# Planned queue orders and slots, and a second Strassen-Winograd level on more of K, in a gated mix of a Fourier transform and a two-layer network

## The chip, the cores and the metric

One core of one Trainium2 chip runs the program. The metric is the device time of one execution in microseconds; lower is better. A time is compared by the median of several runs.

## The reference, cut to what matters

x has 2048 rows (sequence) and 1024 columns; everything is float32.

```python
g = sigmoid((x * gate_w).sum(-1, keepdims=True))
a = x @ dft_hid_re.T ; b = x @ dft_hid_im.T            # 1024 x 1024 each
y = dft_seq_re @ a - dft_seq_im @ b                    # 2048 x 2048 each
h = relu(x @ w1 + b1) ** 2                             # w1 1024 x 3584
o = h @ w2 + b2                                        # w2 3584 x 1024
out = g * y + (1 - g) * o
```

## The kernel before

There are four stages, each a large matrix product: x (the hidden transform, `x_stage`), c (the sequence transform, `c_stage`), h (the first layer in two parts of 16 and 12 tiles of the hidden width, `h_stage(0)` and `h_stage(1)`; the second part works on three-row groups), o (the second layer and the output, `o_stage`). x and h go through `wide`, c and o through `tall`.

**Precision.** A float32 factor is split into a rounded part and the rest: ScalarE writes `hi` (L221), VectorE subtracts it to give `lo` (L231). TensorE then does three matmuls, hi x hi, hi x lo and lo x hi, for each pair of tiles (L307). A row is 128x128 by 128x512. Narrow factors (256 columns) hold both in one block, `both`.

**First level.** Each stage's product is done by Strassen's scheme in Winograd's form: seven products of quarter matrices instead of eight, in the order `(1, 2, 5, 6, 3, 7, 4)`. `FACTORS` names the factors, `SUMS_L` and `SUMS_R` the sums that go into them; VectorE makes these (L173), ScalarE and VectorE evacuate PSUM and add into accumulators (L434, L440, L613, L620).

**Second level.** Some products are split once more (`twice`), others run plainly (`direct`). In `tall` K goes in steps `q` of 256, eight in c and seven in o, and `TWICE_C` and `TWICE_O` say for each product how many couples of steps take the second level; the rest of K goes direct. For a couple of four-row steps, direct is 2 q x 2 halves x 24 matmuls = 96, the second level 7 x 12 = 84. It needs more sums, more hi/lo splits and more evacuations: results of the four groups for the inner products 1, 6, 7 and 5 are added into accumulators (L492 to L531), loaded back into PSUM by ScalarE (L294), and inner products 2, 4 and 3 go on top. In `wide` `TWICE_X` and `TWICE_H` list the products that take the second level as a whole.

**Slots and queues.** SBUF is cut in 55 slots of 128x1024 float32; raw loads, sums, hi, lo and accumulators all take slots from one list. PSUM is cut in four pairs of banks. Each engine runs its queue in order, and a loop over the steps of TensorE writes the orders: at step i it issues loads for up to `LOADS` steps ahead when enough slots are free (`KEEP`, `RAWS`), makes sums and hi parts `SUMS` steps ahead and lo parts `RESTS` steps ahead, goes up to `SPREAD` steps ahead when a small running clock (`MM`, `VEC`, `LAND`, `RATE`) says VectorE would otherwise wait, and puts the last step of an accumulator `LATER` steps behind. SP queues the loads, GpSimd's queue the stores.

Of the kernel before, what the change touches and what calls it, by code (L numbers as in the profile page):

```python
# [14 lines left out]
P = 128  # L15
S, D, F = 2048, 1024, 3584
NF = F // P
SLOTS, KEEP, RAWS = 55, 5, 4
WIDE, TALL_C, TALL_O = ((1, 2, 5, 6, 3, 7, 4),) * 3
TWICE_X, TWICE_C, TWICE_O = (1, 2, 5, 3, 4), {2: 4, 3: 3, 4: 3}, {1: 2, 2: 3, 3: 3, 4: 2}  # L20
LATER = 3
# [3 lines left out]
TWICE_H = (1, 2, 5, 3, 4), (2, 5, 3, 4)  # L25
SUMS, RESTS, LOADS, SPREAD = 3, 2, 12, 9

MM, VEC, ACTS, LAND, RATE = 0.2267, (0.16, 1.067), (0.2, 0.85), 5.0, 1.5
# [14 lines left out]
def gated_mix_kernel(ctx: ExitStack, tc: tile.TileContext, x4, xn, w4, ct, w1a, w1b, w2, b1, b2, gw, out):  # L43
# [11 lines left out]
    nc = tc.nc  # L55
# [4 lines left out]
    free = deque(ctx.enter_context(tc.tile_pool(name=f"slot{i}", bufs=1)) for i in range(SLOTS))  # L60
    banks = deque(ctx.enter_context(tc.tile_pool(name=f"banks{i}", bufs=1, space=bass.MemoryType.PSUM))
                  for i in range(4))
    home = {}
    b1c = const.tile([P, NF], F32, name="b1c")
    z = const.tile([P, 16], F32, name="z")
    g = const.tile([P, 16], F32, name="g")
    b2c = const.tile([P, 8], F32, name="b2c")
    g_far = dram.tile([P, 16], F32, name="g_far")
# [4 lines left out]
    def take(name, dtype=F32):  # L73
        slot = free.popleft()
        t = slot.tile([P, 2, 512], dtype, name=name, tag="block")
        home[id(t)] = slot, t
        return t

    def give(*tiles):
        for t in tiles:  # L80
            free.append(home.pop(id(t))[0])
# [6 lines left out]
    class Near:  # L88
# [9 lines left out]
        def drop(self):  # L98
            give(self.slot)
            self.slot = None  # L100
# [19 lines left out]
    class Kept:  # L120


        def __init__(self, name):
            self.at, self.done, self.left = dram.tile([P, 2, 512], F32, name=name), False, 2
# [7 lines left out]
    class Part(Near):  # L132
# [10 lines left out]
        def room(self):  # L143
            return sum(not isinstance(b, (Near, View)) for b in self.blocks)

# [13 lines left out]
        def extra(self):  # L159
            return 0 if self.room() else 1  # L160

        def time(self):
            return VEC[0] + VEC[1] * self.width / 512 if self.op else 0.0

        def make_parts(self):
# [9 lines left out]
            give(*mine[1:])  # L175
# [13 lines left out]
        def sum(self):  # L189
            run(self.make_parts())  # L190
            return self.time()

        def rest(self):
            return 0.0

    class Operand:
# [6 lines left out]

        def room(self):
            return 0

        def extra(self):
            return (2 if self.width > 256 else 1) - (self.block.uses == 1)
# [15 lines left out]
        def sum(self):  # L224
            run(self.sum_parts())
            return 0.0
# [9 lines left out]
        def rest(self):  # L236
            run(self.rest_parts())
            return VEC[0] + VEC[1] * self.width / 512

        def used(self):  # L240
            self.uses -= 1
            if not self.uses:
                give(*((self.hi, self.lo) if self.width > 256 else (self.both,)))
# [21 lines left out]
    class Group:  # L265
# [11 lines left out]
        def ends(self):  # L277
            return (self.at + 1) % self.k == 0

        def prepare(self):  # L280

            if not all(b.begun for b in self.onto or ()):
                return
            for k in range(len(self.ps), -(-self.rows // self.per)):
                if not banks or self.per == 2 and len(banks) < -(-self.rows // 2) - k:
                    break
                self.pools.append(banks.popleft())
                t = self.pools[-1].tile([P, 2, 512], F32, name="ps", tag="ps")
                self.ps.append(t)
                if self.onto:  # L290
                    n = min(self.per, self.rows - self.per * k)
                    at = self.per * k % 2
                    b = self.onto[self.per * k // 2]
                    nc.scalar.activation(t[:, :n, :], b.slot[:, at:at + n, :], AF.Copy, scale=self.sign)  # L294
                    if self.spend and (self.per == 2 or at):
                        b.drop()

        def run(self, st, mv, by_part=False):
            self.prepare()
# [18 lines left out]
    steps, wanted, count = [], [], {}  # L318

    def step(st, mv, group):  # L320
# [3 lines left out]
        needs = 0  # L324
        count[group] = count.get(group, 0) + 1
        if count[group] % group.k == 0:
            needs += group.done[count[group] // group.k - 1][1]
        wanted.append(needs)

    stores = []  # L330
    later, now = deque(), [0]
    clock = {"pe": 10.0, "vec": 0.0, "dma": 0.0}

    def vec(t):
        clock["vec"] += t
# [77 lines left out]
    def tall(left, right, ksteps, order, second, first, target, final, last=None):  # L413
# [23 lines left out]
        def add(dst, k, ps, ends=False, src=None, sign=1):  # L437
# [3 lines left out]
            vec(VEC[0] + VEC[1])  # L441
# [19 lines left out]
        def twice(p, old, new, ends, drop, sign):  # L461
# [37 lines left out]
            def onward(dst, key, ps):  # L499

                if old:
# [4 lines left out]
                    vec(2 * (VEC[0] + VEC[1]))  # L506
# [16 lines left out]
            def five(_, ps):  # L523
                key = block(1, 1)
                add(new, block(0, 1), ps)
                if old:
# [5 lines left out]
                    vec(2 * (VEC[0] + VEC[1]))  # L532
                    tmp[0, 0].drop()
                    new[key].begun = True
                    if ends and not more:
                        new[key].done = True
                        later.append((now[0] + LATER, lambda: final(new[key], None)))
# [47 lines left out]
    def wide(left, right, rows, order, second, target, final, sign=1, onto_old=False):  # L585
# [30 lines left out]
        def add(dst, k, ps, ends=False, src=None, sign=1):  # L616
# [5 lines left out]
            vec(VEC[0] + VEC[1] * min(2, rows - 2 * k[2]) / 2)  # L622
            near.begun = True
            if ends:
                near.done = True
                later.append((now[0] + LATER, lambda: final(near, None, 1)))
# [100 lines left out]
    class Gate:  # L727
# [5 lines left out]
        def extra(self):  # L733
            return 0

        def room(self):
            return 1

# [8 lines left out]
        def sum(self):  # L747
            nc.vector.scalar_tensor_tensor(flat(self.raw), flat(self.raw), 1.0, flat(gwb.slot), op0=ALU.mult,
                                           op1=ALU.mult, accum_out=z[:, self.t:self.t + 1])
            give(self.raw)  # L750
            return VEC[0] + VEC[1]

        def rest(self):
# [5 lines left out]
            return 0.0  # L759

    class Row(Near):
# [8 lines left out]
        def extra(self):  # L770
            return 0

        def room(self):
            return 1

# [4 lines left out]
        def sum(self):  # L780
            self.done = True
            if not self.less:
                return 0.0
            nc.vector.tensor_scalar(flat(self.slot), flat(self.slot), -1.0, 1.0, op0=ALU.mult, op1=ALU.add)
            return VEC[0] + VEC[1]

        def rest(self):
            return 0.0
# [8 lines left out]
    def c_stage():  # L797
# [8 lines left out]
        def final(dst, ps):  # L806
# [3 lines left out]
            vec(VEC[0] + VEC[1])  # L810
# [8 lines left out]
    def o_stage():  # L819
# [10 lines left out]
        def last(dst, ps, k):  # L830
            i, n, c, rp = to[dst]
            e, t, add = 4 * i + 2 * rp + k, 1024 * n + 512 * c, fetched[i, n, c, rp]
            dst.slot or dst.new()
# [10 lines left out]
        def final(dst, ps):  # L844
            i, n, c, rp = to[dst]
            e, t, add = 4 * i + 2 * rp, 1024 * n + 512 * c, fetched[i, n, c, rp]
            for k in range(2):
# [4 lines left out]
            vec(2.8)  # L852
# [23 lines left out]
    for (i, n, c, rp), e in fetched.items():  # L876
        want(ends[i, n] - 7 + c if (i, n) != (1, 0) else ends[i, n] - 11 + 6 * c, e)
# [4 lines left out]
    n = len(steps)  # L882
    seen = set()
    items = []

    def need(o, k):

        o = o.base if isinstance(o, (View, Half)) else o
        if id(o) in seen or not isinstance(o, (Part, Operand, Gate, Row)):
            return  # L890
        seen.add(id(o))
        for b in [o.block] if isinstance(o, Operand) else getattr(o, "blocks", ()):
            need(b, k)
        o.need = k
        items.append(o)

    for k, (st, mv, _, also) in enumerate(steps):
        for o in (mv, st, *also):
            need(o, k)
    first = items[:4]  # L900
    assert [type(o) for o in first] == [Part, Operand] * 2
    for o in first[:2]:
        o.cuts = [(slice(k, k + 1), slice(0, 512)) for k in range(2)]
    for o in first[2:]:
        o.cuts = [(slice(0, 1), slice(0, 256)), (slice(0, 1), slice(256, 512)), (slice(1, 2), slice(0, 512))]

    w_parts, x_parts = first[0].load_parts(cycle((nc.sync,))), first[2].load_parts(iter((nc.scalar, nc.sync, nc.sync)))
    for parts in (w_parts, x_parts, x_parts, w_parts, x_parts):
        next(parts)
    run(w_parts, x_parts)  # L910
    ones = const.tile([P, P], mybir.dt.bfloat16, name="ones")
    nc.vector.memset(ones, 1.0)
    idle = banks[-1].tile([P, 2, 512], F32, name="ps", tag="ps")
    for _ in range(WARM):
        nc.tensor.matmul(idle[:, 0, :P], ones, ones, start=True, stop=True)
    run(*(o.make_parts() for o in first[::2]), *(o.sum_parts() for o in first[1::2]),
        *(o.rest_parts() for o in first[1::2]))
    for o in first:
        o.landed = 0.0

    def ready(o):
        near = [o.block] if isinstance(o, Operand) else getattr(o, "blocks", ())
        return all(b.done for b in near if isinstance(b, (Near, View)))

    loaded = summed = rested = 4
    for i in range(-SUMS, n + LATER + 2):
        start = clock["pe"] if i >= 0 else 0.0
        if 0 <= i < n:
            clock["pe"] += steps[i][2].rows * 6 * MM
        end = clock["pe"]  # L930
        ahead = sum(wanted[max(i, 0):i + 5]) + sum(o.extra() for o in items[summed:] if o.need <= i + SUMS + 1)
        while loaded < len(items) and items[loaded].need <= i + LOADS:
            o = items[loaded]
            if any(isinstance(b, Kept) and not b.done for b in getattr(o, "blocks", ())):
# [86 lines left out]
```

## Time and profile before

| | |
|---|---|
| three runs | 1882.26, 1885.99, 1886.69 us (median 1885.99) |
| profiled execution | span 1879.6 us from first to last instruction; its time with what lies around the span is not listed apart, the three runs are 2.7 to 7.1 us above the span |
| TensorE busy | 1866.2 us (99%), 8228 matmuls |
| VectorE busy | 1686.0 us (90%), 1638 instructions |
| ScalarE busy | 1044.1 us (56%) |
| granted TensorE clock | 0.999 |
| moved by DMA | 443.97 MB, 236 GB/s over the span |

A page line gives busy time, share of the span and number of instructions. In a line of a group stand line, engine, operation, out<-in, shape and count, then busy time and mean ns of one, then the idle time of the engine just before them with what ended it. In a table by stretch stand the stretch, its length, the busy time and count of TensorE, its weight loads, VectorE, ScalarE and GpSimd, the granted clock, the busy share of the DMA engines and GB/s. In the chain and the timeline stand start, length and what ran. A matmul's end is modelled (0.39 us where the next one starts 0.23 us later), so start times tell its pace.

### The profile page before, as it was taken

How to read it: one execution, taken by the hardware profiler on the slowest of the kernel's cores; microseconds unless marked ns; L12 is line 12 of the kernel's file. 1: busy time of each engine (PE TensorE's matmuls, PEld its weight loads, DVE VectorE, ACT ScalarE, POOL GpSimd, SP SyncE). 2: the span in 40 equal slices, each digit the busy share in tenths (PEclk: the TensorE clock that was granted, in tenths of full speed). 3: DMA queues.
4: the chain of work that ended last, by engine and by line, in shares of the span. 5: the costliest groups of instructions: out<-in, count | busy, mean ns of one | idle time of the engine just before them, and what ended most of it. 6: DMA issues, size and time to landing. Idle time of an engine off the chain costs nothing.

```text
span 1879.6 us, 22035 instructions
## 1 busy us (share of the span) xinstructions
PE 1866.2 (99%) x8228; PEld 1541.3 (82%) x8228; DVE 1686.0 (90%) x1638; ACT 1044.1 (56%) x1184; POOL 87.6 (5%) x162
## 2 busy tenths in 40 slices
PE   9999999999999999999999999999999999999998
PEld 7888888888888878888888888888888888887887
DVE  8997898599779898799996998799999998699898
ACT  6474563363343554366485797676977534264453
POOL 0000110000000000000000010000100000000000
PEclk9999999999999999999999999999999999999999
DMA  6732989439788379464461766536865798638971
GB/s 224 249 121 74 351 286 412 141 112 361 275 307 330 128 299 378 149 232 181 137 221 61 302 234 218 195 122 246 298 233 177 254 389 317 258 124 335 409 256 52
DMA packets 128570, 443.97 MB, mean 236 GB/s; under 512 B 14144, under 2 KB 23632, under 8 KB 128464
## 3 DMA queue, kind: packets, MB, share of 16 engines
q1 hardware_dynamic: 106560, 364.05, 53.7%
q0 software_dynamic: 21616, 78.14, 10.4%
q8 instruction: 64, 1.05, 0.2%
q10 hardware_dynamic: 288, 0.39, 0.1%
q14 instruction: 42, 0.34, 0.1%
HBM read 363.87 MB, written 78.65 MB: 235 GB/s over the span
## 4 chain that ended last, share of the span: by engine, by line
PE 94%; DVE 4%; DMA 1%; ACT 1%; issue 0%; SPq 0%; DVEq 0%; ACTq 0%
PE ps L307 94%; DVE lo L231 1%; DVE h L620 1%; DVE sum L173 1%; DMA raw<-in_x 0%; DVE u L503 0%; DMA raw<-in_w1b 0%; DMA g<-g_far 0%; DVE both L231 0%; DVE raw L173 0%; ACT ps L294 0%; ACT h L717 0%; ACT hi L221 0%; DVE o L505 0%; SPq L153 0%
## 5 line engine op out<-in xcount | busy, mean ns | idle before, releaser
L307 PE MATMUL ps<-hi 128*128 128x512 f32 x2168 | 844.3, 390 | 3.3 <-ACT hi L221 2.7
L307 PE MATMUL ps<-lo,hi 128*128 128x512 f32 x2168 | 844.1, 390 | 0.0
L307 PE MATMUL ps<-hi,lo 128*128 128x512 f32 x2168 | 843.3, 390 | 0.7 <-DVE lo L231 0.6
L221 ACT ACTIVATE hi<-raw 128x1024 fp32r<-128x1024 f32 (+2 forms) x398 | 406.8, 1037 | 370.6 <-DVE raw L173 245.7
L231 DVE TENSOR_TENSOR lo<-raw,hi 128x1024 fp32r<-128x1024 f32 (+2 forms) x398 | 468.3, 1197 | 45.5 <-ACT hi L221 28.4
L307 PEld LDWEIGHTS ps<-hi 128*128 128x128 f32 x2168 | 407.5, 188 | 89.7 <-ACT hi L221 3.5
L307 PEld LDWEIGHTS ps<-hi,lo 128*128 128x128 f32 x2168 | 407.6, 188 | 86.3 <-DVE lo L231 2.1
L307 PEld LDWEIGHTS ps<-lo,hi 128*128 128x128 f32 x2168 | 407.4, 188 | 84.4 <-DVE lo L231 0.4
L173 DVE TENSOR_TENSOR raw<-raw 128x1024 f32<-128x1024 f32 (+1 forms) x276 | 325.6, 1206 | 57.4 <-DMA raw<-in_ct 13.6
L307 PE MATMUL ps<-hi,both 128*128 128x512 f32 x1120 | 347.9, 390 | 3.1 <-ACT ps L294 3.1
L221 ACT ACTIVATE hi<-sum 128x1024 fp32r<-128x1024 f32 (+1 forms) x192 | 196.8, 1038 | 184.5 <-DVE sum L173 170.1
L231 DVE TENSOR_TENSOR lo<-sum,hi 128x1024 fp32r<-128x1024 f32 (+1 forms) x192 | 228.0, 1200 | 31.5 <-PE ps L307 18.2
L307 PEld LDWEIGHTS ps<-hi,both 128*128 128x128 f32 x1120 | 210.3, 188 | 49.4 <-ACT ps L294 5.5
L307 PE MATMUL ps<-lo,both 128*128 128x512 f32 x560 | 218.3, 390 | 0.1
L173 DVE TENSOR_TENSOR sum<-raw 128x1024 f32<-128x1024 f32 (+2 forms) x136 | 140.3, 1048 | 13.0 <-PE ps L307 9.3
L173 DVE TENSOR_TENSOR sum<-raw,sum 128x1024 f32<-128x1024 f32 (+2 forms) x102 | 112.4, 1107 | 13.3 <-PE ps L307 10.3
L307 PEld LDWEIGHTS ps<-lo,both 128*128 128x128 f32 x560 | 105.2, 188 | 22.0 <-DVE lo L231 0.6
L620 DVE TENSOR_TENSOR h<-h,ps 128x1024 f32<-128x1024 f32 x92 | 98.1, 1085 | 9.0 <-ACT u L613 7.0
L613 ACT ACTIVATE u<-ps 128x1024 f32<-128x1024 f32 x76 | 71.8, 952 | 51.6 <-PE ps L307 43.7
L294 ACT ACTIVATE ps<-u 128x1024 f32<-128x1024 f32 x79 | 76.9, 980 | 20.7 <-DVE o L848 7.1
L221 ACT ACTIVATE both<-sum 128x512 fp32r<-128x512 f32 x80 | 49.6, 625 | 58.6 <-DVE sum L173 43.6
L717 ACT ACTIVATE h<-h,b1c 128x512 f32<-128x512 f32 x112 | 74.3, 715 | 10.5 <-DVE h L620 10.2
(62 smaller groups left out, 724.2 us busy)
## 6 DMA issues: line engine op xcount, KB each, us to landing
raw<-in_ct SPq DMA_DIRECT2D x151, 512.0 KB, 6.9
raw<-h SPq DMA_DIRECT2D x134, 512.0 KB, 7.3
raw<-in_x SPq DMA_DIRECT2D x107, 512.0 KB, 4.9
raw<-in_w SPq DMA_DIRECT2D x98, 512.0 KB, 6.9
raw<-ab SPq DMA_DIRECT2D x72, 512.0 KB, 6.6
h<-h POOLq DMA_DIRECT2D x48, 512.0 KB, 5.9
raw<-in_w1a SPq DMA_DIRECT2D x36, 512.0 KB, 5.5
ab<-ab POOLq DMA_DIRECT2D x32, 512.0 KB, 6.4
```

The source lines that it names most:

```text
L173: nc.vector.tensor_tensor(self.slot[:, k, c], src[0][:, k, c], src[1][:, k, c], op=self.op)
L221: nc.scalar.activation(self.hi[:, k, c], self.block.slot[:, k, c], AF.Copy)
L231: nc.vector.tensor_tensor(self.lo[:, k, c], self.block.slot[:, k, c], self.hi[:, k, c].bitcast(F32), op=SUB)
L294: nc.scalar.activation(t[:, :n, :], b.slot[:, at:at + n, :], AF.Copy, scale=self.sign)
L307: nc.tensor.matmul(self.ps[r // self.per][:, r % self.per, :], a[:, kk, r * P:(r + 1) * P], b[:, kk, :], start=self.at == 1 and kk + n == ...
L613: nc.scalar.activation(view(near.slot, k), view(ps, k), AF.Copy, scale=float(sign))
L620: nc.vector.tensor_tensor(view(near.slot, k), view((src or dst)[k].slot, k), view(ps, k), op=ADD if sign > 0 else SUB)
L717: nc.scalar.activation(dst.slot[:, k, :], (dst.slot if ps is None else ps)[:, k, :], AF.Relu, bias=b1c[:, tile0 + k:tile0 + k + 1])
```

## The change

Which products take the second level, and on how many couples:

```diff
-TWICE_X, TWICE_C, TWICE_O = (1, 2, 5, 3, 4), {2: 4, 3: 3, 4: 3}, {1: 2, 2: 3, 3: 3, 4: 2}
+TWICE_X, TWICE_C, TWICE_O = (1, 2, 5, 3, 4), {1: 1, 2: 4, 3: 4, 4: 4}, {1: 2, 2: 3, 3: 3, 4: 3}
-TWICE_H = (1, 2, 5, 3, 4), (2, 5, 3, 4)
+TWICE_H = (1, 2, 5, 3, 4), (1, 2, 5, 3, 4)
```

The loop that wrote the queues is gone, with `KEEP`, `RAWS`, `SUMS`, `RESTS`, `LOADS`, `SPREAD` and `LATER`. The kernel now runs once against recording queues: each operation becomes an `Op` with what it reads and writes, what it must follow, and a duration by constants. Operands are made where a step first needs them; final sums are recorded at once; the gated blocks of the output stage (`fetched`) are loaded where their sum is recorded.

```diff
-MM, VEC, ACTS, LAND, RATE = 0.2267, (0.16, 1.067), (0.2, 0.85), 5.0, 1.5
+MM, MM_END, FIRST_MM = 0.2267, 0.18, 6.2
+VEC, VEC_END, ACT, ACT_END = (0.086, 1.0417e-3), 0.39, (0.11, 0.89e-3), 0.36
+ISSUE, RING, RATE, SEM, LANES = {"sync": 0.36, "scalar": 0.36, "gpsimd": 0.56}, (1.1, 1.1), 400e3, 0.06, 8
+LEAD = {"raw": 5.0, "hi": 5.0, "sum": 5.0, "out": 0.0}
-                later.append((now[0] + LATER, lambda: final(near, None)))
+                final(near, None)
+    def ready(o, engines):
...
+        for b in [o.block] if isinstance(o, Operand) else getattr(o, "blocks", ()):
+            ready(b, engines)
+        store_all()
+        o.load(engines)
+        o.sum()
+        o.rest()
+    for k, (st, mv, group, also) in enumerate(steps):
...
+        ready(mv, cycle((nc.sync,)))
+        ready(st, iter((nc.scalar, nc.sync, nc.sync)) if k == 0 else cycle((nc.sync,)))
...
+        group.run(st, mv, by_part=k == 0)
...
+    emit(tc, plan(ops, len(slots), ideal[0]), slots, pools)
```

`plan` gives each operation a time at which it is due, worked back from TensorE's matmuls at an unbroken pace, and then plays the program through: every engine takes the ready operation that is due first, a slot goes to the block whose first operation is due first less its `LEAD`, loads share one rate, and TensorE keeps its order. `emit` writes the instructions in the order that this gives, and ties each to the one before it on its engine.

```diff
+    for op in reversed(ops):
...
+        length = op.time + op.end + SEM + (op.load + sum(RING) if op.load else 0.0)
+        for o in op.then:
+            op.due = min(op.due, o.due - (op.time if o.engine == op.engine and not op.load else length))
...
+    queue = sorted(((lead(op, b), op.at, b, op) for op in ops for b in op.new if b.home == "slot"), key=lambda e: e[:2])
...
+        while head < len(queue) and free:
+            _, _, b, op = queue[head]
+            b.slot = free.popleft()
...
+                op = ready[e][0][2]
+                if op.load:
+                    lane = lanes[e == "gpsimd"]
+                    if len(lane) >= LANES and not lane[-LANES].landed:
+                        continue
...
+    for op in order:
+        for b in op.new:
+            pool, tag = (slots[b.slot], "block") if b.home == "slot" else (pools[b.bank], "ps")
...
+        if op.engine in last:
+            tc.add_manual_dep(made.ins, last[op.engine].ins.name, mybir.DependencyInfo(
+                mybir.DependencyClass.NoSync, mybir.DependencyReason.DATA), reason="queue order")
```

More of the change, by code (lines that the diff above doesn't have):

```diff
@@ L63, in gated_mix_kernel @@
[L63 to L68, printed above, removed]
+    slots = [ctx.enter_context(tc.tile_pool(name=f"slot{i}", bufs=1)) for i in range(SLOTS)]
+    pools = [ctx.enter_context(tc.tile_pool(name=f"banks{i}", bufs=1, space=bass.MemoryType.PSUM)) for i in range(4)]
+    banks, held = deque(range(4)), [None] * 4
@@ L73, in take @@
     def take(name, dtype=F32):
[L74 to L81, printed above, removed]
+        return Block(name, dtype, "slot")
     def run(*parts):
@@ L275, in __init__ @@
             self.ps, self.pools = [], []
-        def ends(self):
-            return (self.at + 1) % self.k == 0
         def prepare(self):
[L282 to L286, printed above, removed]
+            for k in range(-(-self.rows // self.per)):
                 self.pools.append(banks.popleft())
-                t = self.pools[-1].tile([P, 2, 512], F32, name="ps", tag="ps")
+                t = Block("ps", F32, "bank")
+                t.before, t.bank, held[self.pools[-1]] = held[self.pools[-1]], self.pools[-1], t
                 self.ps.append(t)
@@ L781, in sum @@
             self.done = True
[L782 to L785, printed above, removed]
+            if self.less:
+                nc.vector.tensor_scalar(flat(self.slot), flat(self.slot), -1.0, 1.0, op0=ALU.mult, op1=ALU.add)
         def rest(self):
-            return 0.0
+            pass
         def of(self, c):
@@ L875, in gated_mix_kernel @@
     want(at + 20, *rows)
[L876 to L895, printed above, removed]
@@ L908, in gated_mix_kernel @@
[L908 to L917, printed above, removed]
@@ L918, in gated_mix_kernel @@
[L918 to L934, printed above, removed]
-                break
-            if isinstance(o, Row) and not Row.ready:
-                break
-            if o.need > i + SUMS and (len(free) - o.room() < KEEP + ahead or i < 0):
-                break
-            if o.need > i + SUMS and o.room() + sum(e.room() for e in items[summed:loaded]) > RAWS:
-                break
-            o.load(cycle((nc.sync,)))
-            clock["dma"] = max(clock["dma"], start) + RATE * o.room()
-            o.landed = clock["dma"] + LAND - RATE if o.room() else 0.0
-            loaded += 1
@@ new lines, in gated_mix_kernel @@
+    ideal, t = [], FIRST_MM
+    for st, mv, group, _ in steps:
+        ideal.append(t)
+        t += group.rows * 6 * MM
+    ones = fixed([P, P], "ones", mybir.dt.bfloat16)
+    nc.vector.memset(ones, 1.0)
+    idle = Block("ps", F32, "bank")
+    idle.bank, held[banks[-1]] = banks[-1], idle
+    for _ in range(WARM):
+        nc.tensor.matmul(idle[:, 0, :P], ones, ones, start=True, stop=True)
+    for k, (st, mv, group, also) in enumerate(steps):
+        if k == 0:
+            for o in (mv, mv.block):
+                o.cuts = [(slice(k, k + 1), slice(0, 512)) for k in range(2)]
+            for o in (st, st.block):
+                o.cuts = [(slice(0, 1), slice(0, 256)), (slice(0, 1), slice(256, 512)), (slice(1, 2), slice(0, 512))]
+        ready(mv, cycle((nc.sync,)))
+        ready(st, iter((nc.scalar, nc.sync, nc.sync)) if k == 0 else cycle((nc.sync,)))
+        urgent[0] = ideal[k]
+        for o in also:
+            ready(o, cycle((nc.sync,)))
+        urgent[0] = None
+        group.run(st, mv, by_part=k == 0)
+        st.used()
+        mv.used()
+        store_all()
```

319 lines of the change are left out of this document (224 added, 95 removed).

## The prediction

> **What bounds the kernel now.** I read the page's busy times first, then the chain that ended last, then the busy times by stretch of the span.
>
> ```profile
> span 1879.6 us, 22035 instructions
> PE 1866.2 (99%) x8228; PEld 1541.3 (82%) x8228; DVE 1686.0 (90%) x1638; ACT 1044.1 (56%) x1184; POOL 87.6 (5%) x162
> PE 94%; DVE 4%; DMA 1%; ACT 1%; issue 0%; SPq 0%; DVEq 0%; ACTq 0%
> ```
>
> TensorE is the bound: 99% busy and 94% of the chain. VectorE stands right behind it with 90%. In the chain in order of time (start, length, what), one long piece gives TensorE's pace, and pieces of VectorE's give its own:
>
> ```profile
> 9.61 1.23 DVE sum L173
> 11.97 3.40 DVE sum L173 x3
> 666.23 0.60 DVE both L231
> ...
> 673.24 511.10 PE ps L307 x2252
> 1283.93 0.87 DVE lo L231
> ```
>
> 511.10 over 2252 matmuls is 0.227 us each. A VectorE operation on 128x1024 takes a new start every 3.40/3 = 1.13 us when operations follow each other, one on 128x512 0.60 us, one on 128x768 0.87 us. 8228 matmuls less the 44 warm-up ones are 8184, and 8184 x 0.227 = 1857.8 us. The remaining 21.8 us of the span are start, end and stalls:
>
> ```profile
> 6.04 0.73 PE L307 MATMUL ps<-hi 128*128 128x512 f32 x2
> ...
> 14.74 0.50 PE L307 MATMUL ps<-hi 128*128 128x512 f32 x1 [2.65 <-ACT hi L221]
> ...
> 16.56 0.80 PE L307 MATMUL ps<-hi,lo 128*128 128x512 f32 x1 [0.60 <-DVE lo L231]
> 17.15 0.63 PE L307 MATMUL ps<-hi 128*128 128x512 f32 x1
> 17.58 0.63 PE L307 MATMUL ps<-lo,hi 128*128 128x512 f32 x1
> ...
> 19.29 0.50 PE L307 MATMUL ps<-hi,lo 128*128 128x512 f32 x1
> ...
> 19.85 0.40 PE L307 MATMUL ps<-lo,hi 128*128 128x512 f32 x1
> ...
> 1874.10 0.39 PE L307 MATMUL ps<-hi,both 128*128 128x512 f32 x1
> ```
>
> The first real matmul starts at 6.04 and the last at 1874.10, 5.5 before the end. So 21.8 - 6.0 - 5.5 = 10.3 us are stalls between them. The row at 19.85 is the 37th matmul; 36 x 0.227 = 8.2, so 19.85 - 6.04 - 8.2 = 5.6 us are lost by then and 4.7 after it. Most of those 4.7 show by stretch (length, then busy times of PE, PEld, DVE, ACT, POOL):
>
> ```profile
> 660.00:675.00 15.00, 13.67 (x57) 10.10 (x57) 15.00 (x17) 10.80 (x13) 0.00 (x0) 1.00 0.44 142
> 1690.00:1700.00 10.00, 8.36 (x37) 6.59 (x36) 10.00 (x11) 6.28 (x8) 0.00 (x0) 1.00 0.41 132
> ```
>
> These two stretches hold most of what is left: TensorE idles 1.33 and 1.64 us while VectorE is busy throughout. Both lie where a product with a second level ends its first four groups and their results must be added while operands of the next groups are still missing. So whatever adds VectorE work to such products can cost TensorE time, and whatever removes matmuls gains 0.227 us apiece until VectorE takes over.
>
> **The change part by part.** *Matmuls.* A couple of K done directly in a four-row product costs 2 x 2 steps of 24 matmuls, 96; on the second level it costs seven steps of 12, 84. The four added couples (product 1, 3 and 4 of the sequence transform, product 4 of the output) save 48. Product 1 of h's second part has three rows: 8 steps of 18 become 7 of 18, 18 fewer. Counted in the two built programs it is 8184 against 8118, 66 fewer: 66 x 0.227 = **-15.0 us**, all of it on the path.
>
> *VectorE work.* Counted by shape in the built programs there are 90 operations more: 37 of 128x1024, 46 of 128x512, 7 of 128x768. Durations by shape:
>
> ```profile
> L231 DVE TENSOR_TENSOR lo<-raw,hi 128x1024 fp32r<-128x1024 f32 x369 | 443.3, 1221 | 35.7 <-ACT hi L221 23.9 <-PE ps L307 9.0 <-DMA copy<-raw 1.1
> L231 DVE TENSOR_TENSOR both<-sum,both 128x512 fp32r<-128x512 f32 x80 | 54.7, 688 | 2.3 <-ACT both L221 2.1
> L173 DVE TENSOR_TENSOR raw<-raw 128x768 f32<-128x768 f32 x16 | 15.1, 955 | 4.8 <-DMA raw<-in_w1b 4.8
> ```
>
> 37 x 1.22 + 46 x 0.69 + 7 x 0.955 = 83.6 us busy, so VectorE goes from 1686 to 1770 us in a span that shrinks to about 1864: 95%. On the path this is nothing as long as it lies beside matmuls. Where, is the question. For each product I counted the VectorE operations whose result is first needed in it (at 1.13, 0.60 and 0.87 us), against its matmuls:
>
> ```
> product                      VectorE due, us      matmuls, us
>                              before    after      before    after
> sequence transform, 1          29.5     48.6        87.0     84.3
> sequence transform, 3          86.8     99.1        78.9     76.1
> sequence transform, 4          82.2     90.0        78.9     76.1
> h second part, 1               12.5     30.0        32.6     28.6
> h second part, 4               38.7     43.2        28.6     28.6
> output, 3 (not changed)        86.8     86.8        68.0     68.0
> output, 4                      78.2     86.0        70.7     68.0
> ```
>
> ```profile
> 289.00:871.00 582.00, 580.67 (x2557) 479.63 (x2556) 500.09 (x499) 262.14 (x288) 17.07 (x32) 1.00 0.68 255
> 871.00:1360.00 489.00, 488.43 (x2150) 402.97 (x2149) 442.54 (x418) 356.35 (x432) 31.88 (x60) 1.00 0.57 202
> 1360.00:1874.00 514.00, 512.09 (x2258) 423.34 (x2257) 476.97 (x483) 261.63 (x297) 21.72 (x36) 1.00 0.69 256
> 452.00:626.00 174.00, 174.00 (x769) 144.24 (x768) 141.60 (x127) 65.08 (x66) 9.58 (x18) 1.00 0.80 299
> 626.00:705.00 79.00, 77.67 (x339) 63.12 (x339) 77.92 (x81) 43.78 (x51) 0.64 (x2) 1.00 0.65 234
> 792.00:871.00 79.00, 79.00 (x349) 65.17 (x348) 78.62 (x79) 45.97 (x52) 2.66 (x5) 1.00 0.58 214
> 1148.00:1181.00 33.00, 33.00 (x148) 27.33 (x147) 19.96 (x20) 20.04 (x26) 2.13 (x4) 1.00 0.48 163
> 1332.00:1360.00 28.00, 28.00 (x125) 23.22 (x124) 27.80 (x30) 27.85 (x37) 2.99 (x6) 1.00 0.72 266
> 1651.00:1720.00 69.00, 67.36 (x298) 55.47 (x297) 68.29 (x73) 39.00 (x47) 0.00 (x0) 1.00 0.55 204
> 1796.00:1870.00 74.00, 74.00 (x328) 61.33 (x327) 73.88 (x81) 41.05 (x48) 3.56 (x5) 1.00 0.35 126
> ```
>
> By whole stages (the first three rows: sequence transform, h, output) VectorE's busy time fits: 500 plus about 45 is 545 in 573 us; 443 plus 24 is 467 in 485; 477 plus 9 is 486 in 511. Within a stage the rich products (626, 792, 1332, 1651, 1796) are already full, so their added work must be done ahead, in the poor ones: 452 to 626 has 32 us of VectorE idle. How far ahead the engine can work is shown by the output's product 3: 86.8 us are due in 68.0 us of matmuls, and the stretch 1651 to 1720 held 68.3 busy; so some 18 us had been done before it, and the price was the 1.64 us stall above. After the change, the sequence transform's product 3 needs 99.1 - 76.1 = 23 us ahead, its product 4 14, the output's product 4 18. The nearest row is the output's product 3, so I price each of the six new or enlarged ones at 0 to 2 us, +3 in all; bounds: 0, and the whole overflow, priced under the rivals.
>
> *Queue orders and slots.* The hand-written look-ahead is replaced by one that sorts each queue by the time at which a result is needed and hands out the 55 slots in that order. SP's, ScalarE's, VectorE's and GpSimd's queues are all reordered; TensorE's keeps its order of steps. It can remove at most the 4.7 us of stalls after 20 us and may add its own; I take -2, with -4.7 and +10 (twice what the first 20 us lose, the worst stretch of the trace) as ends, since 3.0 of those 4.7 are the two bursts that stay in kind. ScalarE's 47 added activations cost about 36 us of its 44% idle time, and two more 512 KB loads (6.9 us median to landing on the page) go beside matmuls: nothing. If a load is late, what waits is VectorE's next operation and all behind it:
>
> ```profile
> raw<-in_ct SPq DMA_DIRECT2D x151, 512.0 KB, 6.9
> raw<-gy SPq DMA_DIRECT2D x16, 512.0 KB, 4.4
> ```
>
> The gated values that the last products add (gy) are now SP's last loads, where they were spread before. The last one is needed at the end: one landing, 4.4 us, bounds that from above, 0 from below, and I take 0, since slots come free by then.
>
> ```profile
> 0.00:20.00 20.00, 15.57 (x81) 12.45 (x82) 14.51 (x17) 13.92 (x17) 0.20 (x4) 0.91 0.91 340
> ```
>
> *Start.* SP now queues three whole 512 KB loads before the second piece of the first operand; the first step's matmuls will halt where they ran through. In return, the sums that TensorE waited for at 14.74 and 16.56 are now VectorE's third and fourth operations, where they were the sixth and ninth. Between a halt of up to 4.4 us more (1.5 MB at the row's 340 GB/s) and the about 4 us of the two waits (2.65, 0.60, and the slow matmuls from 17.15 on), I take -1.5.
>
> Sum: -15.0 + 3 - 2 - 1.5 = -15.5 us; 1879.6 - 15.5 = 1864.1 us of span. The three runs (1882.26, 1885.99, 1886.69) lie 2.7 to 7.1 us above this span; with the median's 6.4 the forecast is **1870.5 us**.
>
> **Rivals.** *Slower: the lead isn't had.* VectorE stays as idle in the poor products as it is now, because slots, evacuations or late loads hold it, and the rich ones get all of their own additions. Then those stretches last as long as VectorE's work: 77.9 + 12.3 = 90.2 instead of 79 (product 3 of the transform), 78.6 + 7.8 = 86.4 instead of 79, 73.9 + 7.8 = 81.7 instead of 74, 20.0 + 17.5 = 37.5 instead of 33, 27.8 + 4.5 = 32.3 instead of 28; product 1 of the transform gains its 2.7. That is 11.2 + 7.4 + 7.7 + 4.5 + 4.3 - 2.7 = +32.4, and with the start's -1.5 1917 us. Against the forecast's -15.0 it is a swing of 47.4, so it decides where less than two thirds of the overflow is done ahead. After the gap that ended at 14.74 six matmuls started 0.43 us apart (17.15 to 19.29 above) where 0.227 is the pace, five intervals and 1.0 us lost besides the gap; if each of the five halts comes in one piece and is followed by such matmuls, that is 5 us more, 1922. [...] For it: the rich rows are full already and VectorE idles 32 us in one poor product. Against it: the 18 us lead before 1651.
>
> *Faster: the planning removes what is left.* The stalls after 20 us go, the bursts with them, and the start gains 4: -15.0 - 4.7 - 4 = -23.7, 1862 us. For it: at 1690 VectorE ran operations without a break, so another order among them could have put those first for which TensorE waited. Against it: the rich products are richer.
>
> *The savings are eaten:* one third to two thirds of the overflow isn't done ahead, 1879 to 1886 or so: the same time.
>
> **How the numbers follow.** Forecast, 1864 to 1879: 0.55. Faster rival, 1858 to 1864: 0.21. Eaten: 0.09. Slower rival, up to 1917: 0.13; with the slow matmuls, to 1922: 0.02. A measurement of this kernel can tell 0.3% from no change, 5.7 us: faster is below 1880.3, same up to 1891.6. Faster 0.55 + 0.21 = 0.76; same 0.09; slower 0.13 + 0.02 = 0.15. The range reaches from the fast rival's lower end, 1857, to 1884, within the eaten case, and leaves out the slower rival and a little at both sides.
>
> **What the profile after would show.** Right: 8162 PE instructions, pace 0.227, VectorE about 1770 us busy, TensorE's idle stretches still a few of 1 to 2 us at the ends of second-level groups, and the stretch that was 452 to 626 with markedly less VectorE idle than 32 us. Wrong: a TensorE pace interrupted through the transform's products 3 and 4 or all of h, with VectorE named as releaser while it idled before; or waits on DMA in VectorE's list beyond today's few.

## The result, and the profile after

The changed kernel takes 1871.76 us (median of four runs, 1869.78 to 1873.10) against 1886.34 us (four runs, 1882.26 to 1887.19): a ratio of 0.9926, 95% interval 0.9912 to 0.9939, so 0.7% faster. The 14.6 us between the medians rest on four runs of a kernel that spreads: in its 51 runs listed with the experiments, on three other chips, it took 1879 to 1890 us, with medians of 1882.9 to 1884.6. The forecast was 1870.5 us, within 1857 to 1884.

The page of the changed kernel, first its span and busy times, then VectorE's share by slices:

```profile
span 1869.6 us, 22164 instructions
PE 1852.4 (99%) x8162; PEld 1529.5 (82%) x8162; DVE 1761.1 (94%) x1728; ACT 1086.2 (58%) x1231; POOL 87.6 (5%) x162
DVE  8997998999889899999997999999999998989988
```

66 instructions of TensorE fewer and 90 of VectorE more, as counted. VectorE is busy 1761 us, where 1770 were forecast, and its share rises from 90 to 94%. By stretch (the three stages, then the two products ahead of the transform's product 3, which are poor in VectorE work, that product, and the output's product 3):

```profile
286.00:860.00 574.00, 574.00 (x2534) 475.44 (x2533) 537.22 (x543) 283.06 (x318) 16.54 (x31) 1.00 0.68 257
860.00:1348.00 488.00, 484.27 (x2133) 399.91 (x2133) 466.83 (x442) 367.02 (x438) 31.60 (x59) 1.00 0.57 205
1348.00:1862.00 514.00, 508.87 (x2237) 419.27 (x2236) 489.55 (x499) 272.79 (x311) 23.65 (x39) 1.00 0.70 261
447.00:624.00 177.00, 177.00 (x782) 146.60 (x782) 154.15 (x140) 67.80 (x69) 10.12 (x19) 1.00 0.80 298
624.00:700.00 76.00, 76.00 (x337) 62.95 (x336) 75.14 (x81) 43.53 (x53) 0.56 (x2) 1.00 0.59 219
1640.00:1717.00 77.00, 74.47 (x326) 60.65 (x326) 71.25 (x74) 41.18 (x47) 0.00 (x0) 1.00 0.67 246
```

In the whole sequence transform TensorE is busy 574.00 of 574.00 us: three of the five edits lie here, VectorE does 37 us more than before, and no wait is left, not even the 1.33 us that stood at 660. The product with the most work due (99.1 us in 76) runs through. In exchange h and the output stall more: 3.7 and 5.1 us of visible idle, where it was 0.6 and 1.9.

The span went down by 10.0 us, the median by 14.6. Start times settle where the 10.0 are. At 574.00/2534 = 0.2265 to 0.2266 us a matmul, 66 matmuls are 15.0 us. The first real matmul starts at 6.54 (6.04 before). From there to the last, which started at 1863.83 (1874.10), 8117 intervals at 0.2266 make 1839.3 us, so 18.0 us are stalls, 4.4 of them before 17.1 us and 13.5 after; the same count gives 13.8 for before, 5.7 up to 19.85 us and 8.1 after. The end takes 5.7 (5.5). Sum: -15.0 + 0.5 - 1.3 + 5.4 + 0.2 = -10.2.

Most of the other 4.6 us lies in the kernel before: all its 51 listed runs have 1.8 to 2.1 us around the span, so the span of its median run here was near 1884.3 us and not the profiled 1879.6. A second profile shows where such us can come from.

**before_again**

> The kernel before once more, for a second profile: its runs lie 1879 to 1889 and the profiled one was 1882.3. If the spread comes of stalls that come and go, the span's difference sits in TensorE's stalls after the start; if of what lies around the span, the span is 1879 to 1880 again and the time higher.

It took 1889.0 us with a span of 1887.1: 1.9 us lie around the span (2.2 in the changed kernel), and the span itself is 7.5 us longer than the one first profiled, on another chip. Its output's product 3, by stretch and then in TensorE's timeline:

```profile
1690.00:1702.00 12.00, 8.27 (x34) 5.98 (x33) 12.00 (x13) 9.42 (x14) 0.00 (x0) 1.00 0.36 131
1702.00:1712.00 10.00, 10.00 (x39) 8.08 (x37) 10.00 (x13) 5.74 (x7) 0.00 (x0) 0.83 0.52 172
```

```profile
1698.72 0.50 PE L307 MATMUL ps<-lo,both 128*128 128x512 f32 x1 [1.61 <-DVE lo L231]
1700.98 0.50 PE L307 MATMUL ps<-hi,both 128*128 128x512 f32 x1 [1.75 <-ACT ps L294]
1701.32 0.40 PE L307 MATMUL ps<-lo,both 128*128 128x512 f32 x1
1701.55 0.68 PE L307 MATMUL ps<-hi,both 128*128 128x512 f32 x2
1702.03 0.63 PE L307 MATMUL ps<-lo,both 128*128 128x512 f32 x1
1702.46 1.05 PE L307 MATMUL ps<-hi,both 128*128 128x512 f32 x2
```

In the first profile there was one wait here, of 1.64; now there are two of that size, and the granted clock is 0.83 over the next 10 us, with matmuls 0.43 us apart from 1702.03 to 1705.02. By the count of start times the stretch loses 6.0 us where it lost 1.7. Of the other 3 us of the longer span, half are lost in the first 24 us, the rest in small waits between. So the old queues stood at the edge: in this stretch VectorE has no idle moment to make up a delay; what delayed it is not shown. The profile from which I predicted was of a short run: the 51 spans reach from 1877 to 1888 us.

### The profile page after: what moved, and what is told of

It reads as the page before. It is cut to its first block, busy times and chain, and to the rows that moved or that the text cites. A ratio compares the mean times of both kernels' runs of the same rounds, so it can differ in the third digit from the quotient of the medians.

```text
span 1869.6 us, 22164 instructions
## 1 busy us (share of the span) xinstructions
PE 1852.4 (99%) x8162; PEld 1529.5 (82%) x8162; DVE 1761.1 (94%) x1728; ACT 1086.2 (58%) x1231; POOL 87.6 (5%) x162
## 5 line engine op out<-in xcount | busy, mean ns | idle before, releaser
L1125 PE MATMUL ps<-hi 128*128 128x512 f32 x2034 | 793.5, 391 | 6.5 <-DVE h L1125 2.6
L1125 PE MATMUL ps<-hi,lo 128*128 128x512 f32 x2034 | 792.9, 390 | 1.7 <-DVE o L1125 1.7
L1125 PE MATMUL ps<-lo,hi 128*128 128x512 f32 x2034 | 792.4, 390 | 0.0
L1125 PE MATMUL ps<-hi,both 128*128 128x512 f32 x1344 | 416.1, 390 | 2.5 <-ACT ps L1125 2.5
L1125 ACT ACTIVATE hi<-sum 128x1024 fp32r<-128x1024 f32 x216 | 219.6, 1034 | 157.5 <-DVE sum L1125 111.0
L1125 PEld LDWEIGHTS ps<-hi,both 128*128 128x128 f32 x1344 | 252.3, 188 | 56.1 <-ACT ps L1125 3.8
L1125 DVE TENSOR_TENSOR lo<-sum,hi 128x1024 fp32r<-128x1024 f32 (+1 forms) x216 | 255.1, 1198 | 13.5 <-PE ps L1125 7.4
L1125 PE MATMUL ps<-lo,both 128*128 128x512 f32 x672 | 261.7, 389 | 0.0
L1125 ACT ACTIVATE u<-ps 128x1024 f32<-128x1024 f32 (+1 forms) x116 | 112.2, 972 | 71.4 <-PE ps L1125 53.6
L1125 DVE TENSOR_TENSOR h<-h,ps 128x1024 f32<-128x1024 f32 (+1 forms) x92 | 98.7, 1085 | 8.7 <-ACT u L1125 6.2
L1125 ACT ACTIVATE ps<-u 128x1024 f32<-128x1024 f32 (+1 forms) x84 | 82.1, 980 | 29.2 <-DVE o L1125 7.4
```

The source lines that it names most:

```text
L1125: made = getattr(real[op.engine], op.name)(*(actual(a) for a in op.args), **{k: actual(v) for k, v in op.kwargs.items()})
```

## The experiments

Each edit is to the changed kernel unless said otherwise; ratios are to the kernel before on the same chip. The experiments ran on three other chips, and the changed kernel wasn't run there, so differences to it in us are across chips; the ratios are the safer comparison.

**Which half of the change gains?** Two kernels with one half each.

old_products:

```diff
-TWICE_X, TWICE_C, TWICE_O = (1, 2, 5, 3, 4), {1: 1, 2: 4, 3: 4, 4: 4}, {1: 2, 2: 3, 3: 3, 4: 3}
+TWICE_X, TWICE_C, TWICE_O = (1, 2, 5, 3, 4), {2: 4, 3: 3, 4: 3}, {1: 2, 2: 3, 3: 3, 4: 2}
-TWICE_H = (1, 2, 5, 3, 4), (1, 2, 5, 3, 4)
+TWICE_H = (1, 2, 5, 3, 4), (2, 5, 3, 4)
```

> The planned queues with the couples and products of before (8184 matmuls again). Theory A, the gain is the 66 matmuls and the planned orders bring their own stalls, whatever the products: 15.0 us more than the changed kernel, less about 1.4 us for the stall at 1166 that only the added product of h can cause: about 1885, and the stalls at the ends of h's products and in the output's product 3 stay (11 to 12 us after the start). Theory B, those stalls come of the added VectorE work: they fall to the 8 us of the kernel before or less, so 1880 or below.

1886.95 us, ratio 1.0015 (1.0004 to 1.0026): planned queues without the products gain nothing, they lose 0.15%. Its three stages:

```profile
286.00:870.00 584.00, 584.00 (x2579) 483.55 (x2578) 506.20 (x500) 267.32 (x291) 16.66 (x32) 1.00 0.67 251
870.00:1360.00 490.00, 488.93 (x2151) 403.01 (x2150) 438.53 (x412) 357.54 (x424) 30.95 (x58) 1.00 0.56 203
1360.00:1874.00 514.00, 507.25 (x2230) 417.65 (x2229) 475.47 (x481) 265.85 (x302) 22.93 (x38) 1.00 0.69 259
```

The output's stall is there in full, 6.8 us of visible idle; h's is 1.1. So theory A holds for the output, whose waits are the plan's own, and theory B for part of h: 3.7 us of idle there with all the added products, 1.1 without any.

old_queues, an edit to the kernel before: the five products of the change, and

```diff
-        want(ends[i, n] - 7 + c if (i, n) != (1, 0) else ends[i, n] - 11 + 6 * c, e)
+        want(ends[i, n] - 9 + c if (i, n) != (1, 0) else ends[i, n] - 13 + 6 * c, e)
```

> The old loop that writes the queues, with the added couples and products (8118 matmuls); the loads of the gated blocks are asked for two steps earlier, since the loop otherwise reaches a sum before its load. Theory A: the added work finds room under the old look-ahead too, stalls as before (8 us after the start): 1886.3 - 15.0 = 1871, or some 5 us less than the changed kernel's own stalls would give, 1867. The slower rival of the prediction, the lead isn't had: the stretches of the transform's products 3 and 4, of h's second part and of the output's product 4 last as long as VectorE's work, up to 32 us more than before, 1890 to 1918, TensorE waiting on VectorE's lo there.

1899.08 us, ratio 1.0078 (1.0061 to 1.0096). The same 66 matmuls are gone, and the kernel is slower than before. The poor products and the transform's product 3, then what TensorE waited for (us in total, times, longest):

```profile
457.00:632.00 175.00, 171.81 (x754) 141.86 (x753) 146.93 (x133) 66.22 (x67) 9.05 (x17) 0.99 0.81 299
632.00:716.00 84.00, 80.61 (x336) 64.60 (x335) 82.58 (x90) 44.80 (x54) 1.06 (x2) 0.96 0.55 199
```

```profile
PE ps L307 <- ACT hi L221: 9.0, 5, 2.9
PE ps L307 <- ACT ps L294: 8.8, 8, 1.8
PE ps L307 <- DVE both L231: 3.5, 5, 1.0
PE ps L307 <- DVE y L440: 3.2, 1, 3.2
```

In the transform this is the prediction's slower rival. VectorE idles 28 us in the poor products (23 in the changed kernel), and product 3 lasts 84 us, 82.6 of them VectorE's, where the planned queues need 76. At the end of the output (1814 to 1893) it is so too: VectorE is busy 78.2 of 79 us and TensorE 74.3. But not everywhere: the waits add up to 28.6 us after the warm-up, against 10.5 in the changed kernel, and 18.7 of them end with an operation of ScalarE, among them two in h, of 2.6 and 2.4 us, for a rounding. Not all of the overflow came on top: the rival's full price was 1917.

VectorE does the same work in both, 1758.8 us here and 1761.1 in the changed kernel. What differs is what it waits for: 57 us for transfers and 53 for ScalarE here, 33 and 33 with the planned queues. The two halves are worth +0.15% and +0.78% alone and -0.74% together, so the planning is what makes the products pay. Which part of the planning does it, the order of the queues or that in which the slots are handed out, was not tested apart.

**What makes the stalls that are left?** In the output, TensorE and VectorE of the changed kernel at the end of product 3:

```profile
1706.93 0.39 PE L1125 MATMUL ps<-lo,hi 128*128 128x512 f32 x1
1708.16 0.50 PE L1125 MATMUL ps<-hi,lo 128*128 128x512 f32 x1 [0.85 <-DVE o L1125]
...
1711.57 0.51 PE L1125 MATMUL ps<-hi 128*128 128x512 f32 x1 [0.84 <-DVE o L1125]
...
1715.25 0.51 PE L1125 MATMUL ps<-hi,lo 128*128 128x512 f32 x1 [0.84 <-DVE o L1125]
```

```profile
1707.35 0.75 DVE L1125 SCALAR_TENSOR_TENSOR o<-ps,b2c,g 128x512 f32<-128x512 f32 x1 [0.23 <-PE ps L1125]
1708.02 1.22 DVE L1125 TENSOR_TENSOR raw<-raw 128x1024 f32<-128x1024 f32 x1
1709.15 0.75 DVE L1125 SCALAR_TENSOR_TENSOR o<-ps,b2c,g 128x512 f32<-128x512 f32 x1
```

A step of 12 matmuls fills a pair of banks, six into each. The plan queues the final operation on the first bank (1707.35) for when that bank's six matmuls are done, ahead of the last matmuls of the second bank. Those then wait for it (1708.16), although they touch another bank; I take it that the dependence that the program carries is on the pair, which no trace shows directly. It happens three times, each delaying a matmul by 1.0 us.

whole_bank:

```diff
-                        if (write or wrote or block.home == "bank") and (not box or not sight.box or (
-                                box[0] < sight.box[1] and sight.box[0] < box[1] and (
-                                    block.home == "bank" or box[2] < sight.box[3] and sight.box[2] < box[3]))):
+                        if (write or wrote or block.home == "bank") and (
+                                block.home == "bank" or not box or not sight.box or (
+                                    box[0] < sight.box[1] and sight.box[0] < box[1] and
+                                    box[2] < sight.box[3] and sight.box[2] < box[3])):
```

> The changed kernel, but in the recorded program an operation that touches a pair of PSUM banks follows every earlier matmul into that pair, not only those into its own bank. In the output's product 3 the changed kernel queues the final operation on the first bank of a pair while the last matmuls into the second bank are still to come, and those matmuls then wait for it (three waits of 1.0 us at 1708, 1712 and 1715, releaser VectorE's o). Theory, these waits are made by that order: they go, about 3 us less, 1868.5 to 1869. Rival, VectorE is simply late there: the waits move to the next group and the time stays at 1871 to 1872.

1868.71 us, ratio 0.9917 (0.9898 to 0.9937). The intervals of the two ratios overlap, but the trace decides: both final operations now stand together, no wait on VectorE's o is left, and the output's product 3 runs through (77.00 of 77.00 us).

```profile
1708.45 1.42 DVE L1126 SCALAR_TENSOR_TENSOR o<-ps,b2c,g 128x512 f32<-128x512 f32 x2
1640.00:1717.00 77.00, 77.00 (x342) 63.75 (x341) 73.32 (x77) 42.75 (x48) 0.72 (x1) 1.00 0.66 245
```

In h the changed kernel's longest wait ends with an evacuation (h<-h,ps) that stands behind the making of an operand (lo) in VectorE's queue:

```profile
1194.53 1.22 DVE L1125 TENSOR_TENSOR lo<-raw,hi 128x1024 fp32r<-128x1024 f32 x1
1195.66 1.22 DVE L1125 TENSOR_TENSOR h<-h,ps 128x1024 f32<-128x1024 f32 x1
1197.03 0.47 PE L1125 MATMUL ps<-hi 128*128 128x512 f32 x1 [1.76 <-DVE h L1125]
```

evac_first:

```diff
+EARLY = 3.0
...
+    for op in ops:
+        if op.engine in ("vector", "scalar") and (any(a.base.home == "bank" for a in op.ins + op.outs) or any(
+                a.base.name in ("u", "ab", "y", "h", "o") for a in op.outs)):
+            op.due -= EARLY
```

> The changed kernel, but operations that read or write PSUM on VectorE and ScalarE, and the sums into accumulators, count as due 3 us earlier when the queues are planned. Theory A, the planned order puts operand work ahead of evacuations that TensorE needs first: of the 13.5 us of stalls after the start 7 to 10 go, 1862 to 1865. Theory B, VectorE has no time to spare there: as much is lost again to late operands, 1870 to 1875, with lo as the releaser.

1870.96 us, ratio 0.9926 (0.9911 to 0.9941): nothing gained. The three waits on o remained, and a fourth of 0.84 us came at 1490. The expectation took one cause for all stalls, and for the output's product 3 it was another. With that one mended the edit does gain:

whole_evac, both edits:

> The same, and evacuations count as due 3 us earlier as in the run before. If the two are independent: 0.8 us less than the last one, 1867.5 to 1868.5. If the earlier evacuations only exchange one late operation for another in h, no difference to it.

1865.77 us, ratio 0.9905 (0.9885 to 0.9924), 2.9 us less than whole_bank on the same chip, more than expected. This is the best version found, 1.0% below the kernel before, and the steadiest: its five runs lie within 2 us, the 17 of the kernel before on that chip within 11. By stretch, h and then the start of the output, first whole_bank, then whole_evac:

```profile
860.00:1352.00 492.00, 488.85 (x2150) 402.65 (x2149) 470.43 (x446) 370.08 (x440) 31.49 (x59) 1.00 0.58 207
1352.00:1420.00 68.00, 65.42 (x288) 53.51 (x287) 63.72 (x68) 47.01 (x63) 5.39 (x10) 1.00 0.71 252
860.00:1352.00 492.00, 489.10 (x2151) 403.06 (x2150) 472.41 (x448) 375.30 (x448) 32.84 (x62) 1.00 0.58 210
1352.00:1420.00 68.00, 67.69 (x299) 55.69 (x298) 66.56 (x72) 47.94 (x61) 3.77 (x7) 1.00 0.63 232
```

The gain isn't in h, whose idle goes only from 3.2 to 2.9 us (3.8 in the changed kernel over the same stretch): earlier waits get shorter, and one of 1.50 us comes at its end, at 1349. It lies at the start of the output, where TensorE waited 2.6 us for sums to be loaded back into PSUM (ps, ScalarE) and now waits 0.3.

we_early6, the same with `EARLY = 6.0`:

> The kernel with both repairs, evacuations due 6 us earlier instead of 3. If more of the same helps, the stalls at 1194, 1224 and 1349 (0.4, 0.9, 1.7 us) shrink: 1863 to 1865. If three was enough and operand work now comes late, lo takes the place as releaser: 1866 to 1870.

1868.81 us, ratio 0.9921 (0.9906 to 0.9936): 3 us above whole_evac, by time and by ratio, though the intervals of the two ratios overlap. TensorE's waits:

```profile
PE ps L1131 <- DVE h L1131: 3.2, 3, 1.4
PE ps L1131 <- ACT hi L1131: 2.9, 2, 2.3
PE ps L1131 <- DVE lo L1131: 1.6, 5, 0.8
```

lo appears five times, but the evacuations in h (VectorE's h) still head the list: neither answer is clean. What sets those waits beyond the order of two operations of 1.1 us each stays open.

**The start.** start_first:

```diff
+            self.first = step_now[0] == 0
...
+        step_now[0] = k
...
+    for op in ops:
+        if op.first and op.engine != "tensor":
+            op.due -= 20.0
```

> The changed kernel, but all loads, roundings and differences of the first step count as due 20 us earlier, so that its pieces are queued ahead of the 1.5 MB that stand between them now. If the halts of the first 14 us (matmuls 0.43 us apart and the wait that ends at 10.68) come of that order: 1 to 3 us less, 1869 to 1871. Rival, the first 20 us are bound by the load of all operands of the first three steps or by VectorE: the halts move behind the first step, as at 14.74 in the kernel before, and the time is the same or up to 1 us longer.

1874.19 us, ratio 0.9942 (0.9926 to 0.9958). The first step runs without a halt, and the halt comes behind it:

```profile
11.06 1.07 PE L1131 MATMUL ps<-hi,lo 128*128 128x512 f32 x4
14.68 0.76 PE L1131 MATMUL ps<-hi 128*128 128x512 f32 x1 [2.55 <-ACT hi L1131]
15.24 0.63 PE L1131 MATMUL ps<-lo,hi 128*128 128x512 f32 x1
17.30 0.79 PE L1131 MATMUL ps<-hi,lo 128*128 128x512 f32 x1 [1.43 <-DVE lo L1131]
17.89 0.63 PE L1131 MATMUL ps<-hi 128*128 128x512 f32 x1
```

The rival is right, and by more than it said: two waits and a stretch of matmuls 0.43 us apart, 2.4 us more than the changed kernel has lost by 30 us. Loading the next step's operands first, which looked wrong to me, is the better order of the two.

**How far does it carry?** c1_four:

```diff
-TWICE_X, TWICE_C, TWICE_O = (1, 2, 5, 3, 4), {1: 1, 2: 4, 3: 4, 4: 4}, {1: 2, 2: 3, 3: 3, 4: 3}
+TWICE_X, TWICE_C, TWICE_O = (1, 2, 5, 3, 4), {1: 4, 2: 4, 3: 4, 4: 4}, {1: 2, 2: 3, 3: 3, 4: 3}
```

> The changed kernel with all four couples of the transform's product 1 on the second level: 36 matmuls fewer (8.2 us) and about 32 us more of VectorE work, in products 1 and 2 of the transform. Theory A, planned queues pay for every matmul as long as a stage's VectorE work fits its matmuls (here still 94%): 1863 to 1865. Theory B, what can be done ahead is limited to some 20 us: product 1 no longer has room, products 1 and 2 together hold more VectorE work than matmuls after a product that does too, and the stalls there eat the gain or more: 1871 to 1885.

1884.65 us, ratio 1.0001 (0.9990 to 1.0012): 36 matmuls fewer, 13 us more than the changed kernel (14 by the ratios). The transform's products 1 and 2:

```profile
289.00:370.00 81.00, 74.89 (x310) 59.37 (x309) 80.62 (x100) 45.57 (x57) 1.07 (x2) 0.96 0.67 249
370.00:470.00 100.00, 95.81 (x401) 75.53 (x400) 99.23 (x109) 54.39 (x64) 1.60 (x3) 0.98 0.63 227
```

Over 181 us VectorE is busy 179.9. Here it is the bound, though the stage as a whole has room; two rich products in a row behind the rich last product of the stage before leave no poor one to work ahead in. That is theory B; another order of the products, which would test the reason, wasn't run.

we_c1_two, on top of whole_evac, with `{1: 2, ...}`:

> The kernel of the run with both repairs (pairs of banks as one, evacuations 3 us earlier), with two couples instead of one of the transform's product 1 on the second level: 12 matmuls and 2.7 us fewer, about 12 us more of VectorE work in products 1 and 2 of the transform. Four couples there lost 20 us. If the limit lies between two and four: 2.7 us less than 1865.8, about 1863. If one couple is already at it: stalls of 3 us and more before 450, 1866 to 1872.

1879.43 us, ratio 0.9980 (0.9970 to 0.9990), 14 us worse than whole_evac, and neither expectation named why. One wait makes nearly all of it:

```profile
302.08 0.79 PE L1131 MATMUL ps<-hi 128*128 128x512 f32 x1 [12.89 <-ACT hi L1131]
```

```profile
262.00:302.00 40.00, 27.19 (x120) 22.17 (x119) 36.36 (x46) 12.19 (x12) 4.27 (x8) 0.88 1.02 412
```

At the change of stage the DMA engines are busy throughout (share 1.02, 412 GB/s), as they are there in whole_evac (1.03, 412 GB/s, with TensorE busy 40.00 of 40 us), and TensorE stands until a load of the transform's matrix (in_ct) and its rounding are through. Loads of the rows for the gate's sums stand between those of the matrix in SP's queue. VectorE isn't the limit in this stretch (36 of 40 us, part of it the gate's sums, which nobody waits for yet). That another order of the loads would give the 2.7 us wasn't tried.

we_h_old, whole_evac with h's product 1 direct as before (`TWICE_H = (1, 2, 5, 3, 4), (2, 5, 3, 4)`):

> The kernel with both repairs, but product 1 of h's second part direct as before: 18 matmuls more, 4.1 us. If that edit pays in full: 1869.9. If the stalls of h's second part (4.8 us from 1127 to 1404 in the kernel with both repairs) come of it: they fall to about 3, and the edit is worth only 2 us, 1868. If they come of the planned order whatever product 1 is: the full 4.1.

1870.24 us, ratio 0.9929 (0.9915 to 0.9943), 4.5 us above whole_evac by time and by ratio, though the intervals overlap. With the evacuations due earlier, h idles 2.9 us with or without the edit, so the edit pays its 18 matmuls in full there; the idle comes of the planned order.

## Why the prediction was right, point by point

- *66 matmuls at 0.227, -15.0 us.* Right, on the path entirely: 8162 instructions, the transform busy 574.00 of 574.00.
- *VectorE's work lies beside the matmuls because it can be done ahead.* Right in the transform and the output, and only because of the planning: old_queues has the same work, and TensorE's waits add up to 28.6 us there, against 10.5. The sign named for it came: VectorE's idle time ahead of the transform's product 3 fell from 32 to 23 us.
- *New and enlarged products +3, planning -2.* Wrong in size, and in sign for the planning. Together +1 was forecast, and stalls after the start rose by 5.4 us. The transform's products cost nothing, the low end of the 0 to 2 us each; the bursts at 660 went. But the plan brought waits of its own: three of 1.0 us at the end of the output's product 3, which went with its order there (whole_bank), 2 us at the output's start, and in h evacuations behind operands. With the old products the planned output idles 6.8 us, where the old queues idled 1.9. The step that failed is the -2 for the planning: it counted the old waits that an order could remove, and had no row for the new ones of an order that had never run. Its range, up to +10, held them.
- *4.7 us of stalls after 20 us.* Mis-sized: 0.227 is 0.2266 rounded up, and over 8000 matmuls that hides 3.4 us. It is 8.1.
- *Start -1.5.* -0.8 with the first matmul 0.5 us later. The halt in the first step (1.21 us at 10.68) and the earlier sums both came as described; 2.6 of the 4.4 us that are still lost are matmuls 0.43 us apart.
- *6.4 us around the span.* Wrong: 2.2. The other 4.2 us were a longer span of the median run; that it was stalls, as in the second profile, is likely and not shown for that run. This error and the missed stalls cancel: span 1864.1 forecast, 1869.6 measured, +5.5; surroundings -4.2. The forecast of 1870.5 is closer to 1871.8 than its parts deserve.
- *The slower rival* was refuted for the change. Its mechanism shows in part of old_queues and in c1_four. Its point of decision, two thirds of the overflow, wasn't tested as such.
- *The range.* Its lower end, 1857, is called the faster rival's, which was given as 1858 to 1864; the slip changes nothing.

## What to carry to other kernels

Trading TensorE work for VectorE work pays until one stretch, not the whole, runs out of the second engine (in c1_four VectorE was busy 179.9 of 181 us): sum the work that is due in each stretch, and look for an earlier stretch with idle time and slots to do the excess in. A change of stage can be such a limit by its loads alone (we_c1_two, where TensorE waited 12.89 us with VectorE busy 36 of 40 us). A queue order is part of such a trade: taking away the same 66 matmuls made the program 0.8% slower under the old queues and 0.9% faster under the planned ones (0.9926 against 1.0015). Take several profiles of a kernel that runs at an edge before pricing against one, and compute a pace to four digits where it is multiplied by thousands.

## What the runs showed of the hardware

After some waits TensorE's matmuls started 0.43 us apart instead of 0.23, and the length of one wait alone doesn't decide it. In the second profile of before, waits of 1.61 and 1.75 us with one matmul between them were followed by 0.43 us a matmul, from 1702.03 to 1705.02. One of 1.76 us in the changed kernel (at 1197.03) and one of 1.64 us in the first profile (at 1695.12), each with no other wait in the 3 us before it, were followed by 0.23. The same 0.43 came behind two waits close together in c1_four (2.91 and 1.10 us, from 318.03 to 321.87) and in we_c1_two (12.89 and 1.44 us, from 305.33 to 309.17). It didn't always come at once: after the wait of 2.65 us that ended at 14.74 in the first profile the next three matmuls started 0.23 to 0.35 us apart, and 0.43 us came only behind a second wait, of 0.60 us. Single waits did it too: behind one of 3.19 us in old_queues (at 629.63) the next two starts were 0.59 and 0.43 us on, and after one of 1.92 us in start_first the next matmuls went so:

```profile
1198.88 0.50 PE L1131 MATMUL ps<-hi 128*128 128x512 f32 x1 [1.92 <-DVE h L1131]
1199.19 0.62 PE L1131 MATMUL ps<-lo,hi 128*128 128x512 f32 x1
1199.61 0.63 PE L1131 MATMUL ps<-hi,lo 128*128 128x512 f32 x1
```

What else decides it is open.
